# Moving the q and k transposes of two batches to transposing DMAs, and the state sum of three batches to VectorE

## The chip, the cores and the metric

One core of one Trainium2 chip. The metric is the device time of one launch in microseconds (us), median of several runs. Engines are named as in the profile: PE is TensorE, PEld its weight loads, DVE is VectorE, ACT is ScalarE, POOL is GpSimd, SP is SyncE, which issues the loads.

## The reference

A gated linear attention recurrence (batch 4, 8 heads, 768 steps, head size 48), whose output goes through an MLP mixer:

```python
for t in range(S):
    state = alpha[:, :, t, :, None] * state + np.einsum('bhd,bhe->bhde', k[:, :, t], v[:, :, t])
    y[:, :, t] = np.einsum('bhd,bhde->bhe', q[:, :, t], state)
# x = y as (batch, 768, 384)
xt = x.transpose(0, 2, 1)
h = np.maximum(xt @ w_tok1, 0.0) @ w_tok2
u = x + h.transpose(0, 2, 1)
h2 = np.maximum(u @ w_ch1, 0.0) @ w_ch2
return (u + h2).astype(np.float32)
```

## The kernel before

The recurrence is done in chunks of 128 steps, six to a batch, 24 in all, numbered 0 to 23. A chunk loads four tiles (alpha, k, q, v, 192 KB each). ACT takes the logarithm of alpha, TensorE makes the cumulative sum of it by a triangular matmul, ACT exponentiates it twice, POOL multiplies k and q by the results. TensorE transposes both products, a copy brings them out of PSUM, then follow the scores (`gt`), the state (`su`, `ss`) and the output (`y`). Six chunks give the input of one batch's mixer, which is 186 matmuls or transposes of TensorE per batch.

```python
def e_trk(e):                                   # k: four transposes; e_trq does the same for q
    c["ptp"] = ps_tp_p.tile([128, 8, 128], BF16, name="ps_tp")
    for j in range(4):
        pe.transpose(c["ptp"][:, 4 + j, :], pkk_t[n % NPK][:, 2 * j : 2 * j + 2, :], id128)
...
def e_tp(e):                                    # out of PSUM
    c["tp"] = gtp.tile([128, 8, 128], BF16, name="tp")
    (dve.tensor_copy if e == "DVE" else act.copy)(c["tp"], c["ptp"])
...
def e_su(e):                                    # state: the old one by an identity matmul, plus k'v
    ps = c["s"] = ps_mix_p.tile([128, HD], F32, name="ps_mm")
    if ci > 0:
        pe.matmul(ps[:, 0:HD], lhsT=idd2, rhs=s_prev, start=True, stop=False, ...)
    for j in range(4):
        pe.matmul(ps[:, 96 * j : 96 * j + 96], lhsT=pkk_t[n % NPK][:, 2 * j : 2 * j + 2, :],
                  rhs=c["vb"][:, 2 * j : 2 * j + 2, :], ...)
```

The operations are not issued in the order of the text. The program has a small planner: each operation is given an assumed duration and its dependencies, and the planner picks, engine by engine, what comes next. The outcome is one fixed order of instructions for every engine. So a change of assumed durations, or of the operations, also changes the order of everything else.

## Time and profile before

| | before |
|---|---|
| median (lowest to highest of 3) | 194.31 us (193.26 to 195.12) |
| span of the profiled run | 189.9 us |
| TensorE busy | 168.6 us, 89% |
| DMA packets of the queue of the loads and output stores | 23.6 MB, of 27.0 in all |
| median time of an alpha load, issue to landing | 3.7 us |
| alpha of chunk 12 issued, of chunk 23 issued, the latter landed | 65.3, 111.7, 115.4 us |
| cumulative sum of chunk 23 on TensorE | 116.5 us |

The durations of single matmul rows overlap (below, the row at 74.62 lasts 0.39 us and the next starts 0.22 us after it), so a sum of them says little. What can be added up is the time from the start of one row to the start of the next where they follow each other without a gap. These rows of the timeline of TensorE before (start, length, instruction, operands, count) show it:

```profile
72.98 0.40 PE L324 MATMUL gt_ps<-tp 48*128 48x128 bf16 x8
...
74.62 0.39 PE L307 MATMUL ps_tp<-id_112,pkk_129 128*128 128x128 bf16 x4
74.84 0.33 PE L342 MATMUL ps_mm<-vb,pkk_129 128*128 128x96 bf16 x4
75.01 0.81 PE L492 MATMUL ps_mm<-wc_157,rt 128*128 128x384 bf16 x4
75.66 0.36 PE L362 MATMUL ps_y<-vb,gtm 128*128 128x48 bf16 x8
75.86 0.33 PE L367 MATMUL ps_y<-ss_134,tp 128*128 128x96 bf16 x4
```

From 74.62 to 74.84 four transposes: 0.055 us each. From 74.84 to 75.01 four matmuls of 96 columns: 0.0425 each. From 75.01 to 75.66 four of 384 columns: 0.1625 each. From 75.66 to 75.86 eight of 48 columns: 0.025 each. The scores take 0.041 each (the next row, left out, starts at 73.31), the matmuls of one column 0.026 (four of them 0.10 to 0.11 us). I call these issue slots. Below, **work** of TensorE in a stretch is the number of instructions of each kind times its slot, and **wait** is the rest of the stretch. A time at half clock counts as wait in this way, too.

### The profile page before, as it was taken

How to read it: one execution, taken by the hardware profiler on the slowest of the kernel's cores; microseconds unless marked ns; L12 is line 12 of the kernel's file. 1: busy time of each engine (PE TensorE's matmuls, PEld its weight loads, DVE VectorE, ACT ScalarE, POOL GpSimd, SP SyncE). 2: the span in 40 equal slices, each digit the busy share in tenths (PEclk: the TensorE clock that was granted, in tenths of full speed). 3: DMA queues.
4: the chain of work that ended last, by engine and by line, in shares of the span. 5: the costliest groups of instructions: out<-in, count | busy, mean ns of one | idle time of the engine just before them, and what ended most of it. 6: DMA issues, size and time to landing. Idle time of an engine off the chain costs nothing.

```text
span 189.9 us, 4180 instructions
## 1 busy us (share of the span) xinstructions
PE 168.6 (89%) x1616; PEld 107.5 (57%) x1616; DVE 90.9 (48%) x152; ACT 93.7 (49%) x200; POOL 64.2 (34%) x108
## 2 busy tenths in 40 slices
PE   1377467989999999999979999999999999999992
PEld 0255344456666666657736676655665666566651
DVE  2378547172725676669734896323717102220222
ACT  3534411339885333677777588400664990059000
POOL 3643546006925555795535655500000000000000
PEclk9999955699999999999999999999999999999999
DMA  6999799999999999999999997022200001220122
GB/s 124 226 204 216 143 175 146 198 182 224 191 217 197 195 221 195 200 237 210 243 228 208 190 198 159 2 83 86 83 0 3 0 0 61 104 87 0 59 107 85
DMA packets 107139, 27.00 MB, mean 142 GB/s; under 512 B 100336, under 2 KB 107120, under 8 KB 107120
## 3 DMA queue, kind: packets, MB, share of 16 engines
q1 hardware_dynamic: 103296, 23.60, 58.1%
q0 software_dynamic: 3824, 3.15, 11.1%
q8 instruction: 12, 0.20, 0.4%
q14 instruction: 7, 0.06, 0.1%
HBM read 25.17 MB, written 4.72 MB: 157 GB/s over the span
## 4 chain that ended last, share of the span: by engine, by line
PE 70%; SPq 11%; DMA 8%; issue 3%; POOL 3%; DVE 2%; ACT 2%; POOLq 0%; DVEq 0%; ACTq 0%
PE ps_mm L492 25%; PE ps_mm L474 21%; SPq L230 11%; PE ps_mm L402 5%; PE ps_mm L426 4%; DMA qt<-in_q_dram 3%; PE gt_ps L324 3%; DMA vt<-in_v_dram 2%; DMA at<-in_alpha_dram 2%; PE ps_y L362 2%; PE ps_tp L307 2%; PE ps_mm L447 2%; PE ps_tp L312 2%; PE ps_y L367 1%; POOL pkk_131 L279 1%
## 5 line engine op out<-in xcount | busy, mean ns | idle before, releaser
L384 ACT ACTIVATE rt<-ps_mm 128x384 bf16<-128x384 f32 x90 | 43.2, 491 | 30.2 <-PE ps_mm L474 29.6
L474 PE MATMUL ps_mm<-ut,wc_156 128*128 128x384 bf16 x288 | 54.4, 326 | 0.3 <-DVE ut L455 0.3
L492 PE MATMUL ps_mm<-wc_157,rt 128*128 128x384 bf16 x288 | 49.7, 326 | 0.0
L492 PEld LDWEIGHTS <-rt 128*128 128x128 bf16 x288 | 27.3, 98 | 17.3 <-issue 0.2
L330 DVE TENSOR_TENSOR gtm<-gt_ps,u_107 128x1024 bf16<-128x1024 f32 x24 | 29.3, 1221 | 10.8 <-PE gt_ps L324 10.8
L474 PEld LDWEIGHTS <-wc_156 128*128 128x128 bf16 x288 | 25.9, 97 | 14.8 <-issue 0.8
L504 DVE TENSOR_TENSOR o_sb<-ps_mm,u_sb 128x384 f32<-128x384 f32 x24 | 13.4, 556 | 42.2 <-PE ps_mm L492 41.3
L317 DVE COPY tp<-ps_tp 128x1024 bf16<-128x1024 bf16 x21 | 14.4, 688 | 14.1 <-PE ps_tp L312 13.1
L291 POOL CAST vb<-vt 128x384 bf16<-128x384 f32 x24 | 12.1, 504 | 25.3 <-DMA vt<-in_v_dram 19.4
L375 ACT ACTIVATE x_sb<-ps_y 128x384 bf16<-128x384 f32 x24 | 11.8, 490 | 14.0 <-PE ps_y L367 13.8
L270 ACT ACTIVATE ia_sb<-ps_cum 128x384 f32<-128x384 f32 x24 | 11.8, 491 | 11.7 <-PE ps_cum L264 11.7
L433 DVE TENSOR_TENSOR u_sb<-ps_mm,x_sb 128x384 bf16<-128x384 f32 x24 | 11.8, 550 | 5.2 <-PE ps_mm L426 5.2
L402 PE MATMUL ps_mm<-x_sb,wt_154 128*128 128x384 bf16 x48 | 12.3, 375 | 0.0
L275 ACT ACTIVATE a_sb<-ps_cum 128x388 f32<-128x388 f32 x24 | 11.9, 495 | 0.0
L426 PE MATMUL ps_mm<-ht,wt_155 128*128 128x384 bf16 x48 | 10.6, 328 | 0.6 <-DVE u_sb L433 0.3
L279 POOL TENSOR_TENSOR pkk_131<-kt,ia_sb 128x384 bf16<-128x384 f32 x6 | 6.3, 1048 | 14.2 <-ACT ia_sb L270 14.2
L324 PE MATMUL gt_ps<-tp 48*128 48x128 bf16 x192 | 10.4, 233 | 0.6 <-DVE tp L317 0.4
L362 PE MATMUL ps_y<-vb,gtm 128*128 128x48 bf16 x192 | 9.3, 189 | 1.4 <-DVE gtm L330 1.4
L362 PEld LDWEIGHTS <-gtm 128*128 128x128 bf16 x192 | 8.2, 100 | 3.4 <-DVE gtm L330 2.0
L324 PEld LDWEIGHTS <-tp 48*128 48x128 bf16 x192 | 6.0, 99 | 6.2 <-issue 3.7
L279 POOL TENSOR_TENSOR pkk_130<-kt,ia_sb 128x384 bf16<-128x384 f32 x6 | 6.0, 997 | 8.8 <-ACT ia_sb L270 8.8
L279 POOL TENSOR_TENSOR pkk_129<-kt,ia_sb 128x384 bf16<-128x384 f32 x6 | 6.0, 1002 | 5.5 <-ACT ia_sb L270 5.5
(105 smaller groups left out, 195.5 us busy)
## 6 DMA issues: line engine op xcount, KB each, us to landing
at<-in_alpha_dram SPq DMA_DIRECT2D x24, 192.0 KB, 3.7
kt<-in_k_dram SPq DMA_DIRECT2D x24, 192.0 KB, 3.9
qt<-in_q_dram SPq DMA_DIRECT2D x24, 192.0 KB, 3.8
vt<-in_v_dram SPq DMA_DIRECT2D x24, 192.0 KB, 3.8
out_dram<-o_sb SPq DMA_DIRECT2D x24, 192.0 KB, 1.9
wc_156<-in_moe_w_ch_dram POOLq DMA_DIRECT2D x3, 384.0 KB, 5.9
wc_157<-in_moe_w_ch_dram POOLq DMA_DIRECT2D x2, 576.0 KB, 7.8
wt_154<-in_moe_w_tok_dram POOLq DMA_DIRECT2D x1, 384.0 KB, 6.6
```

The costliest lines, as they stand in the source:

```text
L230: nc.sync.dma_start(c[name], src[b, :, ci * C : ci * C + C, :].transpose([1, 0, 2]))
L279: gps.tensor_tensor(pkk_t[n % NPK][:, :, 0:D], c["kt"], c["ia"], ALU.mult)
L317: (dve.tensor_copy if e == "DVE" else act.copy)(c["tp"], c["ptp"])
L324: pe.matmul(gt[:, 4 * (h % 2) + j, :], lhsT=c["tp"][base : base + D, 4 + j, :], rhs=c["tp"][base : base + D, j, :], start=True, stop=True)
L330: dve.tensor_tensor(c["gtm"], c["gt"], mask_b, ALU.mult)
L362: pe.matmul(ps[:, h, :], lhsT=c["gtm"][:, 4 * (h % 2) + h // 2, :], rhs=c["vb"][:, h, :], start=(h == 0), stop=(ci == 0 and h == H - 1), s ...
L384: act.activation(dst, ps, AF.Relu)
L402: pe.matmul(hold["ps"], lhsT=wt1[:, kc, m * 128 : (m + 1) * 128], rhs=xs[b * NCH + kc], start=(kc == 0), stop=(kc == NS - 1), skip_group_c ...
L426: pe.matmul(hold["ps"], lhsT=wt2[:, kc, i * 128 : (i + 1) * 128], rhs=ht[kc], start=(kc == 0), stop=(kc == NDT - 1))
L474: pe.matmul(hold["ps"], lhsT=wc1[:, kc, mc * 128 : (mc + 1) * 128], rhs=ut_t[0][:, kc, cs], start=(kc == 0), stop=(kc == NM - 1))
L492: pe.matmul(hold["ps"], lhsT=rt[mc][:, i * 128 : (i + 1) * 128], rhs=wc2[:, mc, :], start=(mc == 0), stop=(mc == NDC - 1), skip_group_chec ...
L504: dve.tensor_tensor(hold["o"], hold["ps"], u[i], ALU.add)
```

## The change

The intent is to take work off TensorE. In batches 2 and 3 (12 chunks) eight transposes and the copy out of PSUM are replaced by one transposing DMA of 128x1024 bf16 (`dma_start_transpose`; the prediction calls it the crossbar), issued from ACT's queue. In batches 1 to 3 (12 chunks with a carried state) the identity matmul goes; DVE adds the old state to the product, and DVE or POOL scales it. The core of the diff:

```diff
+    FIRST_DMAT, FIRST_ADD, NKV = 2, 1, 2
...
+            elif o["lands"] and eng == "ACT":          # in the planner: what such a DMA is assumed to take
+                o["end"] = start + 4500.0 + o["lands"]
+                wire += o["lands"]
...
+    pk_t = [fix.tile([128, 2, H, 64], BF16, name=f"pk{i}") for i in range(NPK)]   # q and k side by side
...
+        def e_tpd(e):
+            c["tp"] = gtp.tile([128, 8, 128], BF16, name="tp")
+            nc.scalar.dma_start_transpose(c["tp"], pk_t[n % NPK].rearrange("p a h d -> p (a h d)"))
+        if b < FIRST_DMAT:
             trk = ...; trq = ...; tp = ...             # as before
+        else:
+            tp = plan.op({"ACT": 1250}, e_tpd, [pkk, pkq], -1, takes="tp", frees=[pkk, pkq], lands=950.0)
...
-                if ci > 0:
+                if 0 < ci and b < FIRST_ADD:
                     pe.matmul(ps[:, 0:HD], lhsT=idd2, rhs=s_prev, ...)
...
+            def e_kv(e):
+                dve.tensor_tensor(c["kv"], c["s"][:, 0:HD], s_prev.rearrange("p h d -> p (h d)"), ALU.add)
+            def e_sa(e):
+                (dve if e == "DVE" else gps).tensor_tensor(ss_t[(n - b) % NSS], c["kv"]..., ..., ALU.mult)
```

More of the change, by code (lines that the diff above doesn't have):

```diff
@@ L148 @@
     utpool = pool("utpool", 2)
+    kvp = pool("kvp", NKV)
     rtpool = pool("rtpool", NRT)
@@ L159 @@
                  "ia": NAUX, "pkq": NPK, "pkk": NPK, "vb": NAUX, "acqm": NAUX, "tp": NGT,
-                 "gtm": NGT, "ss": NSS, "x": 18, "ht": 4, "u": 12, "ut": 2, "rt": NRT,
+                 "gtm": NGT, "ss": NSS, "kv": NKV, "x": 18, "ht": 4, "u": 12, "ut": 2, "rt": NRT,
                  "o": 6, "pcum": 1, "ptp": 1, "pgt": 1, "py": 1, "pmix": NMIX}, 36000.0, {"PE": 0.0}, 600.0)
@@ L174 @@
     la_t = [fix.tile([128, H, 64], BF16, name=f"la{i}") for i in range(NLA)]
-    pkq_t = [fix.tile([128, H, 64], BF16, name=f"pkq{i}") for i in range(NPK)]
-    pkk_t = [fix.tile([128, H, 64], BF16, name=f"pkk{i}") for i in range(NPK)]
+    pk_t = [fix.tile([128, 2, H, 64], BF16, name=f"pk{i}") for i in range(NPK)]
+    pkq_t = [t[:, 0, :, :] for t in pk_t]
+    pkk_t = [t[:, 1, :, :] for t in pk_t]
     ss_t = [fix.tile([128, H, D], BF16, name=f"ss{i}") for i in range(NSS)]
@@ L307, in e_trk @@
                 pe.transpose(c["ptp"][:, 4 + j, :], pkk_t[n % NPK][:, 2 * j : 2 * j + 2, :], id128)
-        trk = plan.op({"PE": 215}, e_trk, [pkk], P, takes="ptp", frees=[pkk])
         def e_trq(e):
@@ L312, in e_trq @@
                 pe.transpose(c["ptp"][:, j, :], pkq_t[n % NPK][:, 2 * j : 2 * j + 2, :], id128)
-        trq = plan.op({"PE": 215}, e_trq, [pkq, trk], P - 0.5, frees=[pkq])
         def e_tp(e):
@@ L317, in e_tp @@
             (dve.tensor_copy if e == "DVE" else act.copy)(c["tp"], c["ptp"])
-        tp = plan.op({"DVE": 600, "ACT": 905}, e_tp, [trk, trq], P, takes="tp", frees=[trk])
+        def e_tpd(e):
+            c["tp"] = gtp.tile([128, 8, 128], BF16, name="tp")
+            nc.scalar.dma_start_transpose(
+                c["tp"], pk_t[n % NPK].rearrange("p a h d -> p (a h d)"))
+        if b < FIRST_DMAT:
+            trk = plan.op({"PE": 215}, e_trk, [pkk], P, takes="ptp", frees=[pkk])
+            trq = plan.op({"PE": 215}, e_trq, [pkq, trk], P - 0.5, frees=[pkq])
+            tp = plan.op({"DVE": 600, "ACT": 905}, e_tp, [trk, trq], P, takes="tp", frees=[trk])
+        else:
+            tp = plan.op({"ACT": 1250}, e_tpd, [pkk, pkq], -1, takes="tp", frees=[pkk, pkq],
+                         lands=950.0)
         def e_gt(e):
@@ L331, in chunk @@
         gtm = plan.op({"DVE": 1140}, e_gtm, [gt], P, takes="gtm", frees=[gt])
-        s_prev = ss_t[(n - 1) % NSS]
+        s_prev = ss_t[(n - 1 - b) % NSS]
         s_dep = state.get(n - 1)
@@ L344, in e_su @@
                               rhs=c["vb"][:, 2 * j : 2 * j + 2, :],
-                              start=(ci == 0 and j == 0), stop=(j == 3), skip_group_check=True)
-            su = plan.op({"PE": 330 if ci else 170}, e_su, [pkk, vb, s_dep], P, takes="pmix",
-                         frees=[pkk, vb] + ([s_dep] if ci else []))
+                              start=((ci == 0 or b >= FIRST_ADD) and j == 0), stop=(j == 3),
+                              skip_group_check=True)
+            late = ci > 0 and b >= FIRST_ADD
+            su = plan.op({"PE": 330 if ci and not late else 170}, e_su,
+                         [pkk, vb] + ([] if late else [s_dep]), P, takes="pmix",
+                         frees=[pkk, vb] + ([s_dep] if ci and not late else []))
             def e_ss(e):
@@ L351, in e_ss @@
                 dve.tensor_tensor(
-                    ss_t[n % NSS], c["s"][:, 0:HD].rearrange("p (h d) -> p h d", h=H),
+                    ss_t[(n - b) % NSS], c["s"][:, 0:HD].rearrange("p (h d) -> p h d", h=H),
                     bass.AP(tensor=m.tensor, offset=m.offset,
                             ap=[list(m.ap[0]), list(m.ap[1]), [0, D]]), ALU.mult)
-            state[n] = plan.op({"DVE": 475}, e_ss, [su, acqm], P, takes="ss", frees=[su, acqm])
+            def e_kv(e):
+                c["kv"] = kvp.tile([128, HD], F32, name="kv")
+                dve.tensor_tensor(c["kv"], c["s"][:, 0:HD], s_prev.rearrange("p h d -> p (h d)"),
+                                  ALU.add)
+            def e_sa(e):
+                m = c["acqm"].rearrange("p j h -> p (j h)")
+                (dve if e == "DVE" else gps).tensor_tensor(
+                    ss_t[(n - b) % NSS], c["kv"].rearrange("p (h d) -> p h d", h=H),
+                    bass.AP(tensor=m.tensor, offset=m.offset,
+                            ap=[list(m.ap[0]), list(m.ap[1]), [0, D]]), ALU.mult)
+            if late:
+                kv = plan.op({"DVE": 475}, e_kv, [su, s_dep], P, takes="kv", frees=[su, s_dep])
+                state[n] = plan.op({"DVE": 475, "POOL": 1000}, e_sa, [kv, acqm], P, takes="ss",
+                                   frees=[kv, acqm])
+            else:
+                state[n] = plan.op({"DVE": 475}, e_ss, [su, acqm], P, takes="ss",
+                                   frees=[su, acqm])
         else:
```

## The prediction

> **What bounds the kernel now.** I read the page's busy shares and slices first, then a table of stretches, then the chain that ended last, then single rows.
>
> From the page, busy shares and slices (one digit is a tenth of one fortieth of the span, 4.75 us):
>
> ```profile
> PE 168.6 (89%) x1616; PEld 107.5 (57%) x1616; DVE 90.9 (48%) x152; ACT 93.7 (49%) x200; POOL 64.2 (34%) x108
> ...
> PE   1377467989999999999979999999999999999992
> ...
> ACT  3534411339885333677777588400664990059000
> ...
> PEclk9999955699999999999999999999999999999999
> DMA  6999799999999999999999997022200001220122
> ```
>
> TensorE is full from slice 8 (about 40 us) to its end, at full granted clock, with one dip in slice 20. Before that the kernel waits for its inputs and TensorE partly runs at half clock. The DMA engines are full too, from the start to slice 23 (118 us), and nearly free afterwards. So two resources are full together in the middle and only TensorE in the last third. The stretches (start:end, then busy us and instruction count of PE, PEld, DVE, ACT, POOL; clock, DMA share, GB/s) say the same in numbers:
>
> ```profile
> 66.00:121.00 55.00, 52.33 (x664) 35.74 (x663) 38.40 (x58) 36.96 (x82) 32.38 (x51) 1.00 0.96 199
> 121.00:136.00 15.00, 15.00 (x117) 9.11 (x116) 5.07 (x8) 2.42 (x7) 1.24 (x3) 1.00 0.23 80
> 136.00:187.00 51.00, 50.52 (x332) 30.18 (x328) 12.36 (x22) 22.27 (x46) 0.00 (x0) 1.00 0.11 39
> ```
>
> In 66 to 121 us, while batches 2 and 3 are loaded, TensorE loses only 2.7 us of 55; afterwards nothing but the last 0.5. The chain of waits, in order of time (start, length, what), ends like this:
>
> ```profile
> 139.20 0.74 PE ps_mm L402 x4
> ...
> 147.52 8.29 PE ps_mm L474 x51
> 155.80 11.70 PE ps_mm L492 x72
> 167.50 7.31 PE ps_mm L474 x45
> 174.82 11.71 PE ps_mm L492 x72
> 186.55 0.56 DVE o_sb L504
> ```
>
> The matmuls of 384 columns follow each other every 0.1625 us (11.70 / 72), with no other engine between. Hence any TensorE instruction taken out after 40 us should shorten the end by its issue time, unless the order of the rest begins to wait. These are the pieces that the change takes out, from the same chain (a transpose of k, a transpose of q, the identity matmul needs its row):
>
> ```profile
> 114.74 0.22 PE ps_tp L312 x4
> ...
> 118.43 0.22 PE ps_tp L307 x4
> ```
>
> ```profile
> L339 PE MATMUL ps_mm<-ss_133,idd_119 128*128 128x384 bf16 x8 | 3.0, 377 | 0.0
> ```
>
> [...] in a row four transposes take 0.22 us, 0.055 each; [...] the diff's own planner assumes 1.25 us of ACT, 0.95 us of the DMA engines, and 5.45 us from issue to landing.
>
> **The change, part by part.**
> TensorE, transposes: 12 chunks (batches 2 and 3, six each) x 8 transposes = 96 x 0.055 = 5.3 us out.
> TensorE, state: batches 1 to 3 have four chunks each with a carried state: 12 identity matmuls x 0.1625 = 1.95 us out. Its mean of 377 ns is a pipelined duration; the issue slot counts. Sum on TensorE: 7.2 us, all of it after 60 us, that is, in the full part.
> DVE and ACT, copies: the copy of the transposed pair out of PSUM goes, 12 in all, some nine on DVE and three on ACT:
>
> ```profile
> L317 DVE COPY tp<-ps_tp 128x1024 bf16<-128x1024 bf16 x21 | 14.4, 688 | 14.1 <-PE ps_tp L312 13.1 <-ACT rt L384 0.9
> L351 DVE TENSOR_TENSOR ss_134<-ps_mm,acqm 128x384 bf16<-128x384 f32 x8 | 4.4, 554 | 1.4 <-POOL acqm L297 0.9 <-PE ps_mm L342 0.4
> ```
>
> 9 x 0.69 = 6.2 us off DVE. The new sum of state and product reads PSUM like the row below it, so 12 x 0.56 = 6.7 us on DVE; the scaling after it stays there or moves to POOL (the built order puts five of twelve on POOL at about 1.0 us). DVE is about even, POOL gains 5 us where it is 32.4 of 55 busy. Neither becomes the bound.
> ACT: [...] In 66 to 121 us ACT shows 37 of 55 busy, in durations that overlap; at about 0.39 us from start to start it is nearer 30. [...] The built order moves six more evictions of the hidden layer from ACT to DVE.
> DMA: 12 x 0.95 = 11.4 us of full-rate transfer on top of what is full up to 118 us. In ACT's built order about nine transposes stand before the last chunk's alpha is used, so the loads are delayed by about 9 x 0.95 = 8.6 us.
>
> Does that delay reach the end? Counting the built TensorE order, behind the cumulative sum of the last chunk stand 144 + 24 + 144 = 312 wide matmuls (50.7 us), 18 small transposes (1.0) and two score and three output groups (1.8): 53.5 us. If all 7.2 us are won, TensorE ends at 186.5 - 7.2 = 179.3, so that sum must issue by 125.8. Now the last alpha is issued at 111.7 and takes 3.7, landing at 115.4; delayed by 8.6 it lands at 124.0, the logarithm makes it 124.6. The margin is 1.2 us. The last transpose is as tight: behind its scores stand 282 wide matmuls, so it must have landed by about 132; keys and queries land near 126, two POOL products of 1.0 us each bring 129, a transfer of 4 to 5.5 us brings 133 to 134.5. So I expect 1 to 2.5 us of the 7.2 to come back as waits on TensorE near 120 to 135 us.
>
> Net: 194.3 - 7.2 + 1.5 = 188.6 us.
>
> **The rivals.**
> First, the DMA engines or the transfer's latency take the place of TensorE. For it: share 0.96 up to 121 us, and margins of about 1 us[...]. Against it: the order was planned with 5.45 us of latency and leaves two or more chunks between. At 1.3 us of DMA time each, loads are 11.7 us late and the gain shrinks to about 4 (190 us); at 2 us each it is gone (194 to 196 us).
> Second, ACT's queue becomes the bound: [...] each transposing issue waits for POOL's two products, and behind it stand the exponentials and the evictions that TensorE's three PSUM buffers need. For it: ACT's 7s in slices 16 to 21. Against it: idle gaps of over 1 us before most logarithms there. Each issue that waits 0.5 us extra at a bad place would cost up to 12 x 0.5 = 6 us, more likely 2: 189 to 191 us.
> Third, everything is hidden: the 2.7 us that TensorE now loses between 66 and 121 us also go, since scores no longer follow directly on the transpose and its copy. Then 185 to 186.5 us.
>
> **Range and chances.** A full gain is 187.1, the two waiting rivals put it at 189 to 191, a costly crossbar at 194 and more. A 2% gain needs 190.4. I give 188.6 us, 185.3 to 193.0 for 8 in 10; faster by over 2% 0.64, within 2% 0.30, slower 0.06.
>
> **What would show it.** Right: no transposes of k and q behind 66 us, [...] DMA full until about 128 us, TensorE still at 9s from slice 8 on, losing under 5 us after 66 us. Wrong by DMA: score matmuls waiting for a DMA, or long waits for alpha before the last cumulative sums. Wrong by ACT: hidden-layer matmuls waiting for ACT evictions in 80 to 130 us. The removed part is wrongly sized if TensorE's issue time falls by other than 7.2 us.

## More of the kernel before

The chain of waits by engine on the page of before is what a reader looks at for a bound:

```profile
PE 70%; SPq 11%; DMA 8%; issue 3%; POOL 3%; DVE 2%; ACT 2%; POOLq 0%; DVEq 0%; ACTq 0%
```

It gives 70% to TensorE and 8% to transfers. A chain follows one path only, the one that released last; it doesn't tell how close the next one was.

## The result, and the profile after

The changed kernel is correct and takes **200.64 us** (199.74 to 202.29, 4 runs) beside 194.10 of the kernel before. The ratio is 1.034 (95%: 1.025 to 1.043): 3.4% slower, where 3% faster was expected. Here and below a ratio is the mean time of one kernel's fast runs over that of the other's of the same rounds, so it is not quite the ratio of the medians.

The page of the changed kernel, the rows that answer to those in the prediction (a slice is 4.95 us here):

```profile
PE 167.8 (85%) x1508; PEld 103.8 (52%) x1508; DVE 97.1 (49%) x162; ACT 86.8 (44%) x186; POOL 68.4 (35%) x112
...
PE   1489749999899997567799888999899999999991
...
ACT  3543401278865335335455653113594660098000
...
PEclk9999955999999999995589999999999999999997
DMA  6999899999999898999999999994200002220222
...
q10 hardware_dynamic: 12672, 3.15, 12.1%
...
PE 49%; DMA 22%; SPq 12%; DVE 4%; issue 3%; POOL 3%; ACT 3%; ACTq 1%; POOLq 1%; DVEq 0%
```

108 instructions are gone from TensorE, as planned (1616 to 1508). But slices 15 to 19 (counted from 0; 74 to 99 us) read 75677 where the row of before had 9s, and in slices 18 to 20 (89 to 104 us) the granted clock falls to half. The chain's share of PE fell from 70 to 49%, that of DMA rose from 8 to 22%. The DMA engines are full until the end of slice 26 (134 us); before, it was the end of slice 23, which is 114 us (the prediction wrote 118). ACT, the second rival of the prediction, is busy for 86.8 us against 93.7. That figure leaves out the issuing of transfers: with 12 issues of 1.25 us its queue is occupied for some 102 us, more than before.

The stretches of the changed kernel (us, busy time and count of PE, PEld, DVE, ACT, POOL; clock, DMA share, GB/s). The DMA share comes out above 1 in these rows, so it says that the engines are full and not by how much; the rate is in GB/s:

```profile
66.00:121.00 55.00, 44.84 (x466) 27.25 (x465) 35.06 (x53) 26.31 (x58) 31.88 (x48) 0.91 1.22 215
78.00:90.00 12.00, 6.42 (x72) 3.97 (x72) 8.11 (x14) 3.97 (x8) 8.33 (x13) 1.00 1.24 241
90.00:100.00 10.00, 8.49 (x76) 5.28 (x75) 4.39 (x7) 5.13 (x12) 4.51 (x7) 0.50 1.30 201
```

In 66 to 121 us TensorE is busy for 44.84 us where before it was 52.33. In 78 to 90 us it stands still for nearly half of the time; after that, from 90 to 100 us, it is granted half its clock. What it waits for, from its timeline, and one step back from ACT's:

```profile
84.17 0.32 PE L267 MATMUL ps_cum<-la_127,u_110 128*128 128x384 bf16 x1 [2.09 <-ACT la_127 L261]
...
90.30 0.48 PE L267 MATMUL ps_cum<-la_124,u_110 128*128 128x384 bf16 x1 [2.03 <-ACT la_124 L261]
...
96.28 0.48 PE L267 MATMUL ps_cum<-la_125,u_110 128*128 128x384 bf16 x1 [1.20 <-ACT la_125 L261]
```

```profile
83.60 0.52 ACT L261 ACTIVATE la_127<-at 128x384 bf16<-128x384 f32 x1 [1.82 <-DMA at<-in_alpha_dram]
...
89.73 0.52 ACT L261 ACTIVATE la_124<-at 128x384 bf16<-128x384 f32 x1 [2.55 <-DMA at<-in_alpha_dram]
...
95.71 0.52 ACT L261 ACTIVATE la_125<-at 128x384 bf16<-128x384 f32 x1 [2.63 <-DMA at<-in_alpha_dram]
```

The bracket gives the idle time before a row and what ended it. Each cumulative sum waits for ACT's logarithm, and that for the landing of alpha. The chain of the changed kernel has the same two kinds of transfer in it, the load and the transpose:

```profile
73.92 9.59 DMA at<-in_alpha_dram x2
...
89.36 6.33 DMA at<-in_alpha_dram
...
106.61 6.25 DMA at<-in_alpha_dram
112.98 5.57 DMA tp<-pk_131
```

The transposing transfers themselves behave much as the program's planner had them: 1.25 us of ACT's queue (1.25 assumed), 5.3 us in the median to landing (5.45 assumed).

Now the whole, in work and waits of TensorE between the cumulative sums of chunks 6, 12, 18 and 23 and TensorE's end:

| stretch | before: elapsed = work + wait | after: elapsed = work + wait |
|---|---|---|
| chunk 6 to 12 | 27.9 = 26.9 + 1.0 | 31.9 = 29.5 + 2.4 |
| chunk 12 to 18 | 24.2 = 21.7 + 2.5 | 28.6 = 15.4 + 13.2 |
| chunk 18 to 23 | 21.3 = 18.6 + 2.7 | 33.7 = 29.7 + 4.0 |
| chunk 23 to the end | 69.9 = 68.4 + 1.4 | 56.6 = 53.7 + 2.9 |
| sum | 143.3 = 135.6 + 7.6 | 150.8 = 128.3 + 22.5 |

7.3 us of work were saved, as computed, and 14.9 us of waiting came in, 10.7 of it between chunks 12 and 18 (time lost to the half clock is part of that). The stretch from issuing alpha of chunk 12 to issuing alpha of chunk 23 is the second thing to note: 46.4 us before, 55.9 after. From issue to landing a load of alpha takes 4.5 us in the median, where it took 3.7.

My first theory after this: **loads pace the kernel up to chunk 23**. The DMA engines are full until the last load; the transposes delay the loads; and TensorE's saving before that point is worth nothing, since its next inputs come no sooner. Rivals: the **latency** of a transposing transfer (5.3 us, against 1.1 for eight transposes and their copy: 8 x 0.055 + 0.69) holds the scores; **ACT's queue** is blocked by the 1.25 us issues; the planner's **new order** alone is to blame; and the **clock**, which is granted at half (0.50) from 90 to 100 us, after the waits of 78 to 90.

### The profile page after: what moved, and what is told of

It reads as the page before. It is cut to its first block, busy times and chain, and to the rows that moved or that the text cites.

```text
span 197.9 us, 3963 instructions
## 1 busy us (share of the span) xinstructions
PE 167.8 (85%) x1508; PEld 103.8 (52%) x1508; DVE 97.1 (49%) x162; ACT 86.8 (44%) x186; POOL 68.4 (35%) x112
## 3 DMA queue, kind: packets, MB, share of 16 engines
q10 hardware_dynamic: 12672, 3.15, 12.1%
q0 software_dynamic: 3824, 3.15, 10.7%
## 4 chain that ended last, share of the span: by engine, by line
PE 49%; DMA 22%; SPq 12%; DVE 4%; issue 3%; POOL 3%; ACT 3%; ACTq 1%; POOLq 1%; DVEq 0%
PE ps_mm L528 19%; PE ps_mm L510 17%; DMA at<-in_alpha_dram 15%; SPq L236 12%; DMA qt<-in_q_dram 3%; PE ps_mm L462 3%; DMA tp<-pk_131 3%; PE ps_mm L438 3%; PE ps_mm L483 2%; PE gt_ps L339 1%; PE ps_y L398 1%; ACTq L325 1%; DVE gtm L345 1%; DMA out_dram<-o_sb 1%; POOL pk_130 L289 1%
## 5 line engine op out<-in xcount | busy, mean ns | idle before, releaser
L510 PE MATMUL ps_mm<-ut,wc_155 128*128 128x384 bf16 x288 | 55.5, 334 | 0.7 <-DVE ut L491 0.3
L420 ACT ACTIVATE rt<-ps_mm 128x384 bf16<-128x384 f32 x81 | 39.0, 494 | 20.9 <-PE ps_mm L510 18.1
L510 PEld LDWEIGHTS <-wc_155 128*128 128x128 bf16 x288 | 26.8, 99 | 17.3 <-issue 2.7
L411 ACT ACTIVATE x_sb<-ps_y 128x384 bf16<-128x384 f32 x24 | 11.8, 492 | 25.1 <-PE ps_y L403 22.1
L276 ACT ACTIVATE ia_sb<-ps_cum 128x384 f32<-128x384 f32 x24 | 11.8, 492 | 14.9 <-PE ps_cum L270 11.9
L339 PE MATMUL gt_ps<-tp 48*128 48x128 bf16 x192 | 11.2, 247 | 2.1 <-DVE gtm L345 0.7
L422 DVE TENSOR_SCALAR rt<-ps_mm 128x384 bf16<-128x384 f32 x15 | 8.2, 556 | 8.6 <-PE ps_mm L510 8.6
L321 DVE COPY tp<-ps_tp 128x1024 bf16<-128x1024 bf16 x12 | 8.3, 688 | 8.4 <-PE ps_tp L317 8.4
L398 PE MATMUL ps_y<-vb,gtm 128*128 128x48 bf16 x192 | 9.8, 193 | 2.6 <-DVE gtm L345 2.6
L285 POOL TENSOR_TENSOR pk_130<-kt,ia_sb 128x384 bf16<-128x384 f32 x6 | 6.3, 1043 | 14.5 <-ACT ia_sb L276 14.4
L438 PE MATMUL ps_mm<-x_sb,wt_153 128*128 128x384 bf16 x48 | 11.2, 368 | 0.0
L339 PEld LDWEIGHTS <-tp 48*128 48x128 bf16 x192 | 6.5, 105 | 8.2 <-issue 3.8
L285 POOL TENSOR_TENSOR pk_131<-kt,ia_sb 128x384 bf16<-128x384 f32 x6 | 6.0, 1002 | 11.3 <-ACT ia_sb L276 6.5
```

The costliest lines, as they stand in the source:

```text
L285: gps.tensor_tensor(pkk_t[n % NPK][:, :, 0:D], c["kt"], c["ia"], ALU.mult)
L339: pe.matmul(gt[:, 4 * (h % 2) + j, :], lhsT=c["tp"][base : base + D, 4 + j, :], rhs=c["tp"][base : base + D, j, :], start=True, stop=True)
L398: pe.matmul(ps[:, h, :], lhsT=c["gtm"][:, 4 * (h % 2) + h // 2, :], rhs=c["vb"][:, h, :], start=(h == 0), stop=(ci == 0 and h == H - 1), s ...
L420: act.activation(dst, ps, AF.Relu)
L438: pe.matmul(hold["ps"], lhsT=wt1[:, kc, m * 128 : (m + 1) * 128], rhs=xs[b * NCH + kc], start=(kc == 0), stop=(kc == NS - 1), skip_group_c ...
L510: pe.matmul(hold["ps"], lhsT=wc1[:, kc, mc * 128 : (mc + 1) * 128], rhs=ut_t[0][:, kc, cs], start=(kc == 0), stop=(kc == NM - 1))
```

## The experiments

For each: the edit, what was expected, the outcome. Times are medians in us, beside that of the kernel before on the same chip. Chips differ (193.4 to 196.5 us for the same kernel), so only ratios of the same chip are compared. Work and wait are of the profiled run, from the cumulative sum of chunk 12 to the end; the load stretch is from the issue of alpha of chunk 12 to that of chunk 23.

**1. The two parts alone.** `s_only` has the state part, `t_only` the transposes.

```diff
-    FIRST_DMAT, FIRST_ADD, NKV = 2, 1, 2
+    FIRST_DMAT, FIRST_ADD, NKV = 4, 1, 2      # s_only;  t_only: 2, 4, 2
```

> Only the second part of the change: the state of batches 1 to 3 is added on DVE, all transposes stay on TensorE. It takes 12 identity matmuls of 0.16 us off TensorE (2 us). If the loss of 6 us lies in the transposes, this is 0 to 2 us faster than before (192 to 194 us). If the state's longer chain over DVE and POOL, or the order that comes with it, is to blame, it is 2 us or more slower than before (over 196 us).

> Only the first part: the transposes of batches 2 and 3 by DMA from the ACT queue, the state by the identity matmul. If the transfers are the cause, it is as slow as the whole change or up to 2 us slower (200 to 203 us). If it takes both parts together, or the state part is the cause, it is 192 us or less.

`s_only` 198.97 beside 196.22, ratio 1.015 (1.008 to 1.023); `t_only` 199.87, ratio 1.019 (1.012 to 1.026). Both are correct, and both lose. The two happen to add up to the 3.4% of the whole. The state part has no new transfer, so the transfers are not all of it.

**2. The transfers taken out, and put back as mere traffic.** In `x_none` the scores read the untransposed products, so no transfer is needed; the result is wrong, the order of TensorE is that of the change. In `x_traffic` 12 transposes of a constant tile are added to that, for which nothing waits.

```diff
-            c["tp"] = gtp.tile([128, 8, 128], BF16, name="tp")
-            nc.scalar.dma_start_transpose(c["tp"], pk_t[n % NPK].rearrange("p a h d -> p (a h d)"))
+            c["tp"] = pk_t[n % NPK]...           # a view: x_none
+            nc.scalar.dma_start_transpose(junk_out[n % 3], junk_in)      # x_traffic in addition
```

> The changed kernel with no transposing transfer at all: the score and output matmuls read the untransposed products directly (wrong result on purpose). TensorE's order is the same, instruction by instruction, and so are the waits for the products; DMA traffic, ACT issue time and the transfer's latency are gone. If the transfers in any of their three costs are the cause, the 7.2 us taken off TensorE now show: 186 to 189 us. If the changed order of TensorE is itself at fault, it stays above 194 us.

> As the run without any transposing transfer, but with 12 transposing DMAs of a constant tile into scratch, issued at the same places of the ACT queue (wrong result on purpose): traffic and ACT issue time are back, but nothing waits for their landing. If traffic or ACT issue is the cause, it is as slow as the changed kernel (199 to 201 us); if it is the latency between products and scores, it stays near the run without transfers (186 to 190 us).

`x_none` 195.52 beside 196.22, but three of its four runs are marked slow, being over 1.5% above the one of 191.54, so there is no ratio. The one fast run is 2.4% below the median of before, the slow ones lie near it; whether `x_none` gains anything is not shown. `x_traffic` 203.46, ratio 1.034 (1.024 to 1.043), just that of the change. So the new order with 12 transfers that nobody waits for is as slow as with those that the scores wait for. Latency isn't needed to explain the loss; the load on DMA or on ACT's queue is enough. The chain of `x_none`, in the stretch where TensorE waits, is made almost wholly of alpha loads (its profiled run is one of those marked slow):

```profile
76.03 4.51 DMA at<-in_alpha_dram
...
80.58 3.91 DMA at<-in_alpha_dram
...
85.43 3.98 DMA at<-in_alpha_dram
...
89.53 5.13 DMA at<-in_alpha_dram
```

**3. The order held fixed.** `control` is the changed file with both switches off (same order as before); the runs named `b_` and `s_keep` are built on it. `b_free_keep` keeps that order too: the transposes, copies and identity matmuls of the change's chunks are skipped when emitted, for nothing in their place (wrong), and the state is summed on DVE. `s_keep` does the state part alone in that order (correct). `b_xbar` is the kernel before with 12 useless transposing transfers added.

```diff
         def e_trk(e):                      # b_free_keep; the same in e_trq, and a view in e_tp
+            if b >= 2:
+                return
...
             def e_ss(e):                   # b_free_keep and s_keep, without its identity matmul
+                if ci > 0 and b >= 1:
+                    e_kv(e); e_sa("DVE")
+                    return
...
             (dve.tensor_copy if e == "DVE" else act.copy)(c["tp"], c["ptp"])
+            if b >= 2:                     # b_xbar only
+                nc.scalar.dma_start_transpose(junk_out[n % 3], junk_in)
```

> The changed file with both switches off: every transpose and the state stay on TensorE. All engines' orders are those of the kernel before. Expected: same as before within 0.5%. It gives a trace of the old order on this chip, to set beside the others.

> The order of the kernel before, kept by telling its planner the old costs, but with the transposes of batches 2 and 3, their copies and the identity matmuls of batches 1 to 3 simply left out (scores read untransposed products, wrong result on purpose; the state is added on DVE). No transfer takes their place. If TensorE's issue time sets the end from 40 us on, as I predicted, 7.2 us go: 3.4 to 3.8% faster. If the loads set the pace while they last and only the rest is TensorE's, most of the removed time turns into waiting: 0 to 2% faster.

> Only the state part (identity matmul out, sum on DVE), but in the order of the kernel before. If the loss of the state part alone (1.5% slower in its run) comes from the new order that the planner chose, this is 0 to 1% faster than before; if from the longer chain over DVE itself, it is 1 to 2% slower.

> The kernel before, in its own order, with all its transposes still on TensorE, plus 12 transposing DMAs of a constant tile into scratch from the ACT queue, one per chunk of batches 2 and 3; nothing reads them. Traffic and ACT issue time are added, nothing else. If they cost the loads their DMA time, chunks arrive later and it is 2.5 to 4% slower than before; if they fit into gaps, it is the same within 1%.

Beside 196.51: `control` 197.33, ratio 1.004 (1.001 to 1.007); `b_free_keep` 196.68, ratio 0.998 (0.994 to 1.002); `s_keep` 197.53, ratio 1.005 (1.002 to 1.008); `b_xbar` 207.57, ratio 1.055 (1.046 to 1.064; 2.5 to 4% slower had been expected, too little). `control` itself is 0.4% above before, which the `b_` runs and `s_keep` carry with them.

`b_free_keep` is the sharpest result. All of TensorE's saving, with no transfer and in the very order in which the 7.2 us were counted, is worth nothing against the kernel before. Against `control`, which differs only in what is skipped, it is worth 1.2 us (means: 195.99 and 197.22). In its profile TensorE's work by stretch is 26.2, 18.4, 16.3 and 67.4 us, against 26.9, 21.7, 18.6 and 68.4 in `control`: **only 1.0 us of the 7.3 saved lies behind the cumulative sum of chunk 23.** That is about what was gained. From chunk 12 on the work falls by 6.6 us and the waits rise from 5.8 to 12.7. The load stretch is 47.8 us, in `control` 48.2. The new waits are not all on loads by name: between chunks 12 and 18 they are spread over DVE, POOL and ACT, none above 1.1 us in total, and the clock there is 0.93 in the mean. What shows the pace is the load stretch, which didn't change, and that the DMA engines are full in both. From the sum of chunk 12 to that of chunk 18, first `control`, then `b_free_keep` (columns as above):

```profile
76.30:100.30 24.00, 23.11 (x316) 16.20 (x314) 18.21 (x28) 16.40 (x35) 14.85 (x23) 1.00 1.01 213
```

```profile
75.40:101.50 26.10, 22.02 (x264) 14.25 (x262) 20.47 (x29) 14.57 (x33) 16.27 (x25) 0.93 1.03 215
```

One rival is not tried by an experiment: that SP's issuing, and not the DMA engines, sets the pace of the loads. The traces speak against it. In `control` a late store takes SP 0.33 us to issue and the first load of the kernel 0.43, but an issue in the load stretch takes 0.86 in the mean; in `b_copy` below, where SP has nothing more to issue, it takes 0.99. (In `before` the three are 0.33, 0.42 and 0.84; in `after`, with the transposes, the mean is 1.04.) So in these traces the issues are longer where the DMA engines have more to do. The six input buffers don't hold the loads either: the alpha of chunk 23 takes the buffer of chunk 17, which in `control` was free some 20 us before (sum of chunk 17 at 95.5, alpha of chunk 23 issued at 115.8).

The last landing puts a limit to what any gain elsewhere could have brought: 119.7 in `b_free_keep`, 119.6 in `control`. With the 0.6 us that no sum in these traces goes below, the sum of chunk 23 could start at 120.3; it started at 121.4. Without all the other waits before it, 1.1 us more was to be had.

`s_keep` is as fast as `control` (means 197.23 and 197.22), so the sums on DVE cost nothing that shows, and of the 1.5% that `s_only` lost about one point belongs to the new order (the profile of `s_keep` fell in a slow run). `b_xbar` shows the price of the transfers with their issue on ACT: 10.7 us over the 12 by ratio, 0.9 us each.

**4. What in a transfer costs, the clock, and half of the transfers.** `b_copy` is `b_xbar` with plain copies of the same 256 KB in SBUF; `b_act` has 12 copies by ACT instead and no DMA. `a_warm` puts 120 useless transposes (6.6 us) before the cumulative sums of chunks 13 to 18 of the changed kernel. `t_last` transposes by DMA in batch 3 alone.

```diff
-                nc.scalar.dma_start_transpose(junk_out[n % 3], junk_in)
+                nc.scalar.dma_start(junk_out[n % 3]..., junk_in)      # b_copy
+                act.copy(junk_out[n % 3]..., junk_in)                 # b_act
...
             ps = c["cum"] = ps_cum_p.tile([128, HD + 8], F32, name="ps_cum")
+            if 13 <= n <= 18: ...                                     # a_warm, ahead of it
+                for j in range(20): pe.transpose(warm[:, j % 8, :], id128, id128)
...
-    FIRST_DMAT, FIRST_ADD, NKV = 2, 1, 2
+    FIRST_DMAT, FIRST_ADD, NKV = 3, 1, 2                              # t_last
```

> As the kernel before plus 12 useless transfers from the ACT queue, but plain copies of the same 256 KB (128 rows of 2 KB, memory to memory within the core) in place of transposing ones. If any extra bytes cost the loads alike, it is 4 to 6% slower than before, as with the transposing ones (5.5%). If the transposing form is what is dear, it is 1 to 3% slower.

> As the kernel before plus 12 useless copies of 128x1024 on ACT itself at the same places, about 1.0 us each, and no transfer. If ACT's issue time of 1.25 us each is the cost, it is 3 to 5% slower than before; if the DMA time is, it is the same within 1%.

> The changed kernel with 120 useless 128x128 transposes added on TensorE (6.6 us of issue), 20 ahead of each cumulative sum of chunks 13 to 18, into the PSUM bank that the change leaves free. If TensorE's work sets the time, it is 6 us slower than the changed kernel (about 7% over before). If TensorE waits for loads there anyway, it costs 0 to 2 us, and if the halved clock after the long waits is a real loss, it even gains 1 to 3 us (2 to 3% over before).

> The changed kernel with only batch 3 transposed by DMA (6 transfers instead of 12). If each transfer delays the loads by about 0.9 us, it lies between the state part alone (1.5% over before) and the whole change (3.4%): 1 to 2.5% slower than before. If the loss comes from the first transfers only, at the start of batch 2, it is as fast as before or faster.

Beside 193.43: `b_copy` 199.10, ratio 1.030 (1.022 to 1.037); `b_act` 195.50, ratio 1.011 (1.005 to 1.018); `a_warm` 201.92, ratio 1.045 (1.037 to 1.052); `t_last` 199.70, ratio 1.032 (1.024 to 1.040).

The queue of the added transfers on the page of `b_xbar`, then of `b_copy` (packets, MB, share):

```profile
q10 hardware_dynamic: 12672, 3.15, 11.5%
```

```profile
q10 hardware_dynamic: 1728, 3.15, 4.4%
```

The same 3.15 MB go in seven times as many packets when they are transposed, take 2.7 times the packet time (11.5% of a span of 204.2 us against 4.4% of 197.5), land after 5.4 us in the median against 3.9, and cost 5.5% where plain copies cost 3.0%. Plain transfers of the same bytes thus make over half of the price. The rest is not separated: it can be the longer packet time, or ACT's issue, which takes 1.27 us in `b_xbar` against 0.47 in `b_copy`. Keeping ACT busy for a similar time (12 copies of 1.05 us, against issues of 1.25) costs 1.1%. In `a_warm`, 6.6 us of extra work for TensorE gave a ratio about one point above that of the change, though the intervals overlap; by the traces the stretch from chunk 12 to 18 grew by 1.8 us only (30.4 after 28.6). Work is largely free in that stretch, just as taking it away was. The dip of the clock shrank from 10 to 7 us only, so what the half clock costs by itself isn't told by this run. `t_last` was a miss: half of the transfers, nearly the whole loss. Its profile says why: its load stretch is between the two, 51.5 us, but its order leaves 68.1 us of work behind the last cumulative sum where the change leaves 53.7, so a delayed load goes straight to the end.

**5. Room for the loads, and the planner's assumption.** `b_light` and `a_light` leave out the 12 q loads of batches 2 and 3 (k stands in; wrong) in the kernel before and in the changed one. `a_replan` tells the planner that a transfer keeps the DMA engines for 1.55 us instead of 0.95. `a_late` has the six output stores of batch 0 depend on the last load.

```diff
         def emit(e):                       # b_light, a_light
+            if name == "qt" and b >= 2:
+                c[name] = c["kt"]
+                return
...
-                         lands=950.0)
+                         lands=1550.0)     # a_replan
...
     mixer(B - 1)
+    for st in held:                        # a_late: the stores of batch 0
+        st["deps"].append(loads[NT - 1]["vt"])
```

> The kernel before, in its own order, with the 12 loads of q in batches 2 and 3 left out (k is used for q, wrong result on purpose): about 11 us less work for the DMA engines. If the loads set the pace with TensorE close behind, only the waits go: 1 to 3% faster than before.

> The changed kernel in its own order with the same 12 loads left out; the 12 transposing transfers take about the DMA time that they leave. If the DMA engines' time is what the change lost on, the taken-off 7.2 us of TensorE now show: 3 to 5% faster than before, and faster than the run without q loads alone. If ACT's queue, the latency or the order is at fault, it stays slower than before.

> The changed kernel, with its planner told that a transposing transfer holds up the loads for 1.55 us in place of 0.95, so that it puts the sums of late chunks behind more of the mixer's matmuls. If a good part of the loss is an order made for loads that come too early, it is 1 to 2.5% slower than before in place of 3.4%; if the DMA time itself is the loss, it stays at 3 to 4%.

> The changed kernel with the six output stores of batch 0 held back until the last load has landed (right result): about 5 us of DMA time leave the stretch in which the loads run. If DMA time sets the pace there, the changed kernel gets 1.5 to 2.5% faster, so 1 to 2% slower than before; if not, it stays at 3 to 4%.

Beside 196.39: `b_light` 192.62, ratio 0.982 (0.976 to 0.989); `a_light` 197.09, ratio 1.001 (0.997 to 1.004); `a_replan` 205.78, ratio 1.054 (1.048 to 1.059); `a_late` 203.38, ratio 1.040 (1.035 to 1.045).

Fewer loads make the kernel before 1.8% faster, so loads were part of its bound; but the last alpha lands 12 us sooner than in `control` (107.8 against 119.6) and only 3.8 us come of it by medians: by then TensorE, with 108.7 us of work from chunk 12 on and 4.7 of waits, is the bound. The two were nearly even. The changed kernel gains more from the same room, 3.3 points, but I had expected it to end 3 to 5% faster than before, and it only draws level. The chain of `a_light` tells what holds it then:

```profile
78.88 6.43 DMA tp<-pk
...
88.36 6.17 DMA tp<-pk
```

Once loads come early, the latency of the transposes is on the path, with the exponentials and POOL's products between one and the next; it is 47% of the chain between 74 and 101 us. So the latency rival isn't wrong, it is hidden behind the loads (though these are not out of the way in `a_light`: its load stretch is 45.7 us, against 38.2 in `b_light`). `a_replan` falls: the larger assumption gave an order that was slower still (waits 24.7 us from chunk 12 on; load stretch 59.0). It was no nearer to the truth, either: in the changed kernel the load stretch grew by 0.95 us for each transposing transfer issued in it (9.5 us, ten transfers), just what the planner had assumed. I have not followed why. `a_late` got a new order by its edit, too, and settles nothing.

**6. Stores moved, orders untouched.** `b_defer` issues the six stores of batch 0 behind the last load from the same queue; `a_defer` does it in the changed kernel. Both are correct.

```diff
         def e_st(e, i=i, hold=hold):
+            if b == 0:
+                held.append((out[b, i * 128 : (i + 1) * 128, :], hold["o"]))
+                return
...
             nc.sync.dma_start(c[name], src[b, :, ci * C : ci * C + C, :].transpose([1, 0, 2]))
+            if n == NT - 1 and name == "vt":
+                for dst, o_sb in held:
+                    nc.sync.dma_start(dst, o_sb)
```

> The kernel before with the six stores of batch 0's output issued behind the last load in place of between the loads of batches 2 and 3; TensorE's order is untouched, and the result right. About 5 us of DMA time leave the stretch in which loads and TensorE are both nearly full. If the loads' pace is what holds TensorE there, 0.5 to 2% faster than before; if TensorE's own issue time or the vector engines hold it, the same.

> The changed kernel with the same six stores held back, its order untouched. If DMA time is its loss, it gains more than the kernel before does: 2 to 3% off its 3.4%, so 0.5 to 1.5% slower than before. If it gains no more than the kernel before, the rest of the loss is in the order and the other engines.

Beside 194.50: `b_defer` 192.90, ratio 0.993 (0.989 to 0.997; one of its 11 runs took 564.39 us and is an outlier whose reason I do not know); `a_defer` 204.63, ratio 1.052 (1.046 to 1.058). `b_defer` is the fastest correct version found, by less than 1%: its load stretch is 43.2 us, its last alpha lands at 113.3, and TensorE then has the same tail. `a_defer` shortens the stretch from chunk 12 to 18 from 28.6 to 25.6 us, as the theory of full DMA engines says, and then loses more elsewhere. Its timeline shows where:

```profile
130.39 1.06 DVE L544 TENSOR_TENSOR o_sb<-ps_mm,u_sb 128x384 f32<-128x384 f32 x2 [6.89 <-DMA out_dram<-o_sb]
```

The next mixer's results wait for output buffers that the deferred stores still hold. As a test of the changed kernel it is inconclusive.

**The runs side by side.** From the trace of each profiled run:

| program | DMA transfers added | load stretch | last alpha lands | end of TensorE | work + wait from chunk 12 on |
|---|---|---|---|---|---|
| before | 0 | 46.4 | 115.4 | 186.4 | 108.7 + 6.6 |
| `control` | 0 | 48.2 | 119.6 | 190.8 | 108.7 + 5.8 |
| `b_free_keep` | 0 | 47.8 | 119.7 | 190.3 | 102.1 + 12.7 |
| `s_only` | 0 | 48.9 | 120.6 | 193.5 | 104.1 + 13.0 |
| `x_none` (a run marked slow) | 0 | 47.6 | 119.7 | 190.2 | 98.8 + 14.6 |
| `t_last` | 6 | 51.5 | 122.3 | 194.7 | 101.5 + 18.7 |
| `b_copy` | 12 plain | 54.5 | 123.2 | 193.6 | 108.7 + 12.0 |
| after | 12 | 55.9 | 128.7 | 193.4 | 98.8 + 20.1 |
| `t_only` | 12 | 57.0 | 130.2 | 193.6 | 103.5 + 17.4 |
| `x_traffic` | 12 | 57.1 | 131.8 | 197.8 | 98.8 + 22.1 |
| `b_xbar` | 12 | 57.7 | 128.8 | 200.3 | 108.7 + 19.4 |
| `b_light` | 0, 12 loads less | 38.2 | 107.8 | 186.7 | 108.7 + 4.7 |

The third column carries the explanation. Without added transfers the loads of 11 chunks (44 loads, and six stores between them) take 46.4 to 48.9 us, whether TensorE has 102.1 or 108.7 us of work (98.8 in `x_none`) and in whichever order. Twelve transposes, nine or ten of which are issued within the stretch, make it 55.9 to 57.7. Taking transfers away shortens it, 12 loads in `b_light` (38.2, 11 of them in the stretch) and six stores in `b_defer` (43.2). Per load or store that is 0.96 us in `control`, and 0.98 in `b_light` and `b_defer`. In the order of before, what follows the last landing takes 70.4 to 71.5 us, with transfers or without (before, `control`, `b_free_keep`, `b_copy`, `b_xbar`: last alpha landed to end of TensorE). Where the loads come sooner it takes longer (`b_defer` 73.4, `b_light` 78.9), since TensorE is then not ready for them.

That the last landing sets when the rest begins holds for the order of before only. In the changed order the cumulative sum of chunk 23 stands behind so much other work that it starts at 136.8, 8.1 us after its alpha landed. There the loads hold TensorE up to chunk 22: in this trace no sum starts sooner than 0.6 us after its alpha landed, those of chunks 14 to 17 and 20 to 22 start 0.6 to 0.9 us after, and the alpha of chunk 22 lands at 122.8 (before: 111.8). From its sum on (123.7; before: 113.8) 69.7 us follow to the end of TensorE (before: 72.6). So 9.9 us are lost up to there and 2.9 won behind it, which is the 7.0 us between the ends of TensorE (193.4 and 186.4). It also says that the half clock from 90 to 100 us cost little: by chunk 20 TensorE was again as close behind the loads as anywhere in this trace (0.6 to 0.9 us).

## Why the prediction was wrong

**The step that failed** is the sentence "Hence any TensorE instruction taken out after 40 us should shorten the end by its issue time, unless the order of the rest begins to wait", and with it the term of 7.2 us in the net. The sizes in it were right: the work fell by 7.3 us. But the prediction had itself written that "two resources are full together in the middle and only TensorE in the last third", and then counted savings in the middle at full value. Where DMA is as full as TensorE (in `control`, from chunk 12 to 18, a DMA share of 1.01 beside TensorE's 23.11 us of 24.00), a saving on TensorE became waiting. `b_free_keep` shows it with neither a transfer nor a new order in the way: 1.0 us of the saving lies behind the last load's cumulative sum, the rest became waiting, and the time is that of before, 1.2 us below `control`. The clause "unless the order of the rest begins to wait" named the way out, and the prediction tested it at a single point, the last chunk.

**The cost of the transfers** was the second miss, in what it was charged at. The delay of the loads was estimated at 8.6 us, nine transposes of 0.95 (the planner's assumption; no run had shown it then), with the last alpha landing at 124.0. Measured: the load stretch grew by 9.5 us with ten transposes issued in it, which is 0.95 each, the last alpha was issued 10.7 us later (122.4 after 111.7), took 6.3 us in place of 3.7, and landed at 128.7. That is the mechanism right and the size a little low. But it was set against a margin of 1.2 us computed backward from the end, with TensorE assumed to run full until then, and so came to "1 to 2.5 us of the 7.2". In the change TensorE had fallen behind long before: the waits came at 78 to 100 us, not "near 120 to 135 us", and the cumulative sum of chunk 23 was issued at 136.8 instead of 125.8. By then its alpha had been there for 8.1 us; the test at the last landing looked at the wrong load. Added as mere traffic to the old order, the transfers cost 10.7 us (`b_xbar`).

**The new order and the state part.** The prediction had no term for the order itself. `s_only` shows 1.5% lost, `s_keep` in the old order nothing beyond what `control` shows. (DVE was to come out about even; it is busy for 97.1 us after 90.9. The scaling, counted as before at 0.55 us, takes 0.87 in the mean in `b_free_keep`, where DVE does all twelve.) In the new order more of the work is done ahead of chunk 12 (29.5 us in the stretch before it, against 26.9), so less is left to fill the load-paced stretch behind it: 15.4 us of work against 21.7. That this is what costs the point is my reading of the table; no run isolates it.

**The rivals.** The first, DMA or latency in TensorE's place, happened, and both of its halves are real: the loads' delay is the bound, the transposes' latency comes next to it (`a_light`). Its range, 190 to 196 us, was too low, because it started from a full gain. The second, ACT's queue, did not: an issue took 1.25 us, as the planner had assumed, and TensorE's long waits at 78 to 100 us lead through ACT to a load. But the 2 us that the prediction thought likely for it are about what `b_act` shows for such time on ACT (1.1%), so it is part of the price, and not the bound. The third, all hidden, did not.

**What stays open:** what the half clock between 90 and 100 us costs by itself (little, by the reading of the trace above, but no run isolates it); why `a_replan`'s order is worse; how the price of a transposing transfer divides between the transfer itself and ACT's longer issue; what the new order gains with the transfers free (`x_none` had one fast run); and what would be left of the loss with both light loads and no latency in the new order, for which no run was made.

## What to carry to other kernels

When two resources are full in the same stretch, a saving on one is worth only what lies beyond the stretch: find the event that ends the other's part (in the order of before the landing of the last alpha), add up the work behind it, and count only that (in `b_free_keep` 1.0 us of 7.3). A new order can move that event (here to the load of chunk 22), so look for it again in the order that will run. Moving work onto the resource that is also full can charge its whole time to the end, even if each transfer is small and nobody waits for it: in `b_xbar` both the load stretch (57.7 after 48.2) and the end of TensorE (200.3 after 190.8) are 9.5 us above `control`. And where a planner fixes the order, test a saving with the order held still and with it free, since the new order can cost something by itself: about one point of `s_only`'s 1.5%.
